# Splitting the routed experts' weights: one copy and one subtraction per chunk, all on ScalarE and VectorE

## The chip, the cores and the metric

The kernel runs on one core of a Trainium2 chip, as one program. The metric is the device time of one execution in microseconds (us), the median of several runs. Traces come from the chip's own profiler, one execution each.

## What is computed

Three layers run one after the other on 2304 tokens of width 512, all in float32: attention with a positive feature map, a dense feed-forward layer, and eight routed experts of which each token takes one. The last matters here:

```python
    expert_idx = np.argmax(logits, axis=1)
    ...
    for e in range(E):
        mask = expert_idx == e
        ...
        h = np.maximum(x[mask] @ w1[e], 0.0)
        out[mask] = gate_w[mask, None] * (h @ w2[e])
```

`w1` is 8 x 512 x 1024 and `w2` is 8 x 1024 x 512.

## The kernel before

**Precision.** TensorE takes operands in a shorter float format (fp32r). To keep float32 accuracy, each operand is split into a rounded part *hi* and the rest *lo* = value - hi, and a product is summed from hi x hi, hi x lo and lo x hi. ScalarE makes hi with a copy that rounds, and a second engine makes lo with a subtraction.

**Stages.** Attention and the first half of the dense layer run block by block (nine blocks of 256 tokens), then the second half of the dense layer, whose blocks also compute the router's scores and pick an expert for each token (`y_half_b`, `route`). From about 610 us on the routed experts run (`run`, `step`). The last routing steps and the building of the late tiles' lists (`make_list`, `list_ids`, `list_tail`) are hooked in between the experts' first steps, since the first five expert tiles come from the tokens that were routed early.

**Tiles and chunks of the experts.** Tokens are sorted by expert into tiles of 128 rows; 23 tiles run in the plain loop, and a further loop for rare distributions follows in a branch. The weights of a tile's expert come in four chunks of 128 x 2048 floats (1 MB): chunks 0 and 1 hold `w1` (used by `up`), chunks 2 and 3 hold `w2` (used by `down`). Each chunk number has one buffer, `raw[c]`. `load_w` (line 805) fills it by an indirect DMA issued on GpSimd's queue (line 797), under a branch that skips the load where the tile has the same expert as the tile before. The load of chunk c for tile i + 1 is issued at the end of `split` of chunk c of tile i, because only then is the buffer free.

**The split (lines 822 to 842).** For each chunk, `split` takes a pair of tiles (hi, lo) out of six pairs that rotate over three pools, and works in two halves of 1024 elements a partition: a ScalarE copy (line 837) for hi, then the subtraction (line 839) for lo. The second half's subtraction goes to GpSimd for chunk 3 of every tile and for chunk 2 of tiles 0, 1 and 2 (`I_POOL`, `C_POOL`, lines 59 and 60); all other halves go to VectorE. The chunks are split in the order (i, 0), (i-1, 2), (i, 1), (i-1, 3), as `chunk_of` gives them.

**A step (line 929).** One tile's step on TensorE: `up(i, 0)` (12 matmuls, as `up(i, 1)` and each `down`), `down(i-1, 0)`, `hT(i, 0)`, `up(i, 1)`, the transposes of the next tile's tokens (`xT`), `down(i-1, 1)`, `hT(i, 1)`; a `split` stands between each two of them. After `up`, ScalarE's relu writes `hs` (line 889); `hT` transposes it on TensorE, ScalarE copies the result (line 899) and VectorE subtracts (line 900). `xT` has such a copy and subtraction as well (lines 790 and 791). GpSimd issues the gather of the next tokens (line 777) and the scatter of results (line 922).

**What orders the work.** TensorE's order is the order of the code (a hand-made schedule), and ScalarE's too in the first two steps. On all other queues a planner places the instructions ahead of time by the times that it assumes; on the chip each engine then works through its list in that order, and an instruction that waits holds up all that stand behind it on its engine.

Of the kernel before, what the change touches and what calls it, by code (L numbers as in the profile page):

```python
# [9 lines left out]
F32 = mybir.dt.float32  # L10
# [45 lines left out]
MAN = (mybir.EngineType.PE,)  # L56
ENDS = (0, 1)
TAILS = ((1, 1), (1, 2), (2, 0), (2, 1))
I_POOL = (0, 1, 2)
C_POOL = (2,)  # L60


@with_exitstack
def tile_attention_moe_router_experts(ctx, tc, qT, kT, va, w_phi, moew, emb, embT, tau, ew, out):
    nc = tc.nc
# [9 lines left out]
    def bc(ap, shape):  # L75
        return ap.to_broadcast(shape)
# [14 lines left out]
    for i in range(2):  # L91
        for r in range(2):
            nc.vector.tensor_copy(
                out=wblk[r * D:(r + 1) * D, i, r * F:(r + 1) * F],
                in_=wstk[r * D:(r + 1) * D, i, :].bitcast(F32),
# [362 lines left out]
    def b_load(j):  # L458
# [23 lines left out]
        out=upper, in_=upper, pattern=[[1, P]], compare_op=ALU.is_gt, fill=0.0, base=0, channel_multiplier=-1  # L482
# [4 lines left out]
    def iota_f(shape, pattern, base_, cm, name):  # L487
# [16 lines left out]
        out=lt8, in0=bc(io8.unsqueeze(2), [P, NE, NE]),  # L504
# [265 lines left out]
    raw = [m1.tile([P, 2048], F32, name=f"raw{c}", bufs=1) for c in range(4)]  # L770
# [34 lines left out]
    def load_w(i, c):  # L805
        if i == 0 or i >= N_PLAIN:
            load_rows(i, c)
            return
        if i not in need:
            need[i] = nc.values_load(  # L810
                lists[i][2], engines=[mybir.EngineType.Pool], min_val=0, max_val=3 * NE
            )
        with tc.If(need[i] < NE):
            load_rows(i, c)

    def chunk_of(k):
        i, s = divmod(k, 4)
        return ((i, 0), (i - 1, 2), (i, 1), (i - 1, 3))[s]
# [3 lines left out]
    def split(k):  # L822
        i, c = chunk_of(k)
        if not span[0] <= i < span[1]:
            return
        n = (k - 2 if k > 3 else k // 2) % 6
        if n == 2:
            pool, tag = xg, "xb"
        elif n == 5:
            pool, tag = ring_c, "W"  # L830
        else:
            pool, tag = ring_b, "W"
        hi = pool.tile([P, 2048], F32R, tag=tag, name="whi")
        lo = pool.tile([P, 2048], F32R, tag=tag, name="wlo")
        for h in range(2):
            hs_ = slice(h * 1024, (h + 1) * 1024)
            nc.scalar.copy(out=hi[:, hs_], in_=raw[c][:, hs_])  # L837
            eng = nc.gpsimd if h == 1 and (c == 3 or (i in I_POOL and c in C_POOL)) else nc.vector
            eng.tensor_sub(lo[:, hs_], raw[c][:, hs_], hi[:, hs_].bitcast(F32))  # L839
        wt_[i, c] = (hi, lo)  # L840
        if i + 1 < span[1]:
            load_w(i + 1, c)
# [86 lines left out]
    def step(i, t0, t1, at):  # L929
        live, prev, more = i < t1, i > t0, i + 1 < t1  # L930
        at(i, 0)
        if 4 * i + LEAD > 3:
            split(4 * i + LEAD)
        if more:
            gather(i + 1)
        if live:
            up(i, 0)
        at(i, 1)
        split(4 * i + 1 + LEAD)
        if prev:  # L940
            down(i - 1, 0)
        if live:
            hT(i, 0)
        at(i, 2)
        split(4 * i + 2 + LEAD)
        if live:
            up(i, 1)
        if more:
            xT(i + 1)
        at(i, 3)  # L950
        split(4 * i + 3 + LEAD)
        if prev:
            down(i - 1, 1)
            finish(i - 1)
        if live:
            hT(i, 1)
# [98 lines left out]
```

## Time and profile before

| | |
|---|---|
| runs before | 957.13, 959.81, 960.24 us, median 959.81 |
| profiled execution | 959.22 us |
| its span, first to last instruction | 957.4 us |
| mean granted TensorE clock | 0.974 |
| busy: TensorE, VectorE, ScalarE, GpSimd | 890.8, 732.1, 571.9, 347.8 us |

The engines are called PE (TensorE), DVE (VectorE), ACT (ScalarE), POOL (GpSimd). A row of a timeline has the start in us from the begin of the span, the length, the engine, the line of the code, the operation, what it writes and reads, how many equal instructions are merged in it, and in brackets how long the engine had been idle and what ended that. The releaser in brackets is inferred, and a wait for several things names the last one only. PEclk is the granted clock as a share of the full one.

### The profile page before, as it was taken

What the parts mean: (1) busy time and instruction counts of PE and PEld (TensorE: products, weight loads), DVE (VectorE), ACT (ScalarE), POOL (GpSimd) and SP (SyncE); (2) the same over time, 40 slices, a digit from 0 to 9 for tenths busy, and PEclk for the clock granted to TensorE, in tenths of its full rate; (3) what the DMA queues carried; (4) which work ended last, traced back from release to release, by engine and by line L of the source; (5) the groups of instructions that cost most, each with busy time, mean ns of one, the idle gap of its engine ahead of it and who ended that gap; (6) DMA issues with size and microseconds to landing.
All of it is one profiled execution on the core that took longest, in us unless ns stands there. A gap on an engine that the chain in (4) does not pass through costs nothing. (4 is left out here: it accounts for less than half of the span.)

```text
span 957.4 us, 18720 instructions
## 1 busy us (share of the span) xinstructions
PE 890.8 (93%) x7144; PEld 763.1 (80%) x7144; DVE 732.1 (76%) x1413; ACT 571.9 (60%) x1048; POOL 347.8 (36%) x267
## 2 busy tenths in 40 slices
PE   7778999999999899789999999997889999999994
PEld 6657988898888788669888898885768887888873
DVE  8998676575746544896888889999988877888860
ACT  6865665474645544553333333477679888988861
POOL 0242122031211311563233224526653666644740
PEclk9879999999999999999999999999899999999998
DMA  8665432232221211563222223412541469411650
GB/s 282 195 185 192 147 85 92 80 116 84 78 91 35 101 67 58 183 211 143 89 89 89 88 89 130 190 34 67 191 184 45 145 210 347 147 38 36 220 186 6
DMA packets 43757, 120.68 MB, mean 126 GB/s; under 512 B 4686, under 2 KB 23246, under 8 KB 36624
## 3 DMA queue, kind: packets, MB, share of 16 engines
q1 hardware_dynamic: 33424, 61.48, 19.8%
q0 software_dynamic: 10160, 57.94, 17.4%
q8 instruction: 57, 0.93, 0.4%
q14 instruction: 36, 0.29, 0.1%
q10 hardware_dynamic: 80, 0.03, 0.0%
HBM read 95.84 MB, written 24.90 MB: 126 GB/s over the span
## 5 line engine op out<-in xcount | busy, mean ns | idle before, releaser
L336 PE MATMUL y<-W,gg 128*128 128x512 f32 x864 | 229.5, 399 | 2.7 <-ACT yt L344 1.6
L839 DVE TENSOR_TENSOR wlo<-raw,whi 128x1024 fp32r<-128x1024 f32 x158 | 201.5, 1307 | 39.3 <-ACT whi L837 39.3
L837 ACT CAST whi<-raw 128x1024 fp32r<-128x1024 f32 x184 | 183.8, 1051 | 52.5 <-DMA raw<-in_ew_dram,lwi 16.2
L336 PEld LDWEIGHTS y<-W,gg 128*128 128x128 f32 x864 | 152.6, 189 | 31.4 <-DVE gg L325 2.1
L315 PE MATMUL h<-xb,W 128*128 128x256 f32 x576 | 166.4, 291 | 11.8 <-DVE g L321 8.0
L316 PE MATMUL h<-xb,W 128*128 128x256 f32 x576 | 164.2, 286 | 0.7 <-DVE xb L269 0.7
L317 PE MATMUL h<-xb,W 128*128 128x256 f32 x576 | 163.5, 285 | 0.0
L227 POOL PARTITION_ALL_REDUCE qmx<-pr x28 | 56.7, 2029 | 210.4 <-ACT pr L209 203.0
L315 PEld LDWEIGHTS h<-xb,W 128*128 128x128 f32 x576 | 109.9, 192 | 22.6 <-DVE g L321 12.0
L316 PEld LDWEIGHTS h<-xb,W 128*128 128x128 f32 x576 | 110.5, 192 | 6.1 <-DVE xb L269 1.3
L317 PEld LDWEIGHTS h<-xb,W 128*128 128x128 f32 x576 | 110.5, 192 | 0.8
L319 ACT ACTIVATE t<-h 128x256 f32<-128x256 f32 x144 | 54.2, 381 | 93.1 <-PE h L317 92.6
L323 ACT CAST gg<-g 128x256 fp32r<-128x256 f32 x144 | 57.3, 404 | 83.9 <-DVE g L321 82.7
L563 DVE CUSTOM_DVE_ANT_0 jk<-ys,enb 128x512 f32<-128x512 f32 x128 | 104.9, 820 | 1.9
L325 POOL TENSOR_TENSOR gg<-g,gg 128x256 fp32r<-128x256 f32 x72 | 58.9, 823 | 123.6 <-ACT gg L323 120.1
L321 DVE TENSOR_TENSOR g<-h,t 128x256 f32<-128x256 f32 x144 | 59.7, 418 | 46.0 <-ACT t L319 44.6
L839 POOL TENSOR_TENSOR wlo<-raw,whi 128x1024 fp32r<-128x1024 f32 x26 | 63.9, 2458 | 58.0 <-ACT whi L837 56.1
L304 POOL TENSOR_TENSOR W<-w,W 128x512 fp32r<-128x512 f32 x32 | 44.6, 1398 | 99.7 <-ACT W L303 99.4
L882 PE MATMUL hps<-whi,xt 128*128 128x512 f32 x184 | 77.2, 420 | 0.0
L912 PE MATMUL yo<-whi,h 128*128 128x512 f32 x184 | 75.4, 410 | 0.0
L913 PE MATMUL yo<-wlo,h 128*128 128x512 f32 x184 | 73.3, 398 | 0.0
L883 PE MATMUL hps<-wlo,xt 128*128 128x512 f32 x184 | 73.2, 398 | 0.0
(212 smaller groups left out, 1742.9 us busy)
## 6 DMA issues: line engine op xcount, KB each, us to landing
wst<-in_moew_dram SPq DMA_DIRECT2D x32, 512.0 KB, 4.8
qraw<-in_q_dram SPq DMA_DIRECT2D x36, 256.0 KB, 3.0
xs_d<-xb SPq DMA_DIRECT2D x9, 1024.0 KB, 4.6
xb<-xs_d POOLq DMA_DIRECT2D x9, 1024.0 KB
kraw<-in_k_dram SPq DMA_DIRECT2D x16, 288.0 KB, 3.7
yp_d<-yt SPq DMA_DIRECT2D x9, 512.0 KB, 2.9
yt<-yp_d SPq DMA_DIRECT2D x9, 512.0 KB, 3.8
y_d<-ys SPq DMA_DIRECT2D x18, 256.0 KB, 2.2
```

What stands on the lines that cost most here:

```text
L315: nc.tensor.matmul(hp, w[:, 0, ks], x[:, 0, k, :], start=(k == 0), stop=False)
L316: nc.tensor.matmul(hp, w[:, 0, ks], x[:, 1, k, :], start=False, stop=False)
L317: nc.tensor.matmul(hp, w[:, 1, ks], x[:, 0, k, :], start=False, stop=(k == 3))
L321: nc.vector.tensor_tensor(out=g, in0=hp, in1=t, op=ALU.max)
L336: nc.tensor.matmul(yps[j][t], gg[:, a, ts], w[:, b, DM:2 * DM], start=(c0 == 0 and a == 0 and b == 0), stop=(c0 == NCH - 1 and a == 1),)
L563: nc.vector.tensor_tensor_reduce(out=jk2, in0=ys, in1=enb[:, e, :], scale=1.0, scalar=0.0, op0=ALU.mult, op1=ALU.add, accum_out=lgr[:, t, ...
L837: nc.scalar.copy(out=hi[:, hs_], in_=raw[c][:, hs_])
L839: eng.tensor_sub(lo[:, hs_], raw[c][:, hs_], hi[:, hs_].bitcast(F32))
L882: nc.tensor.matmul(ps, x[:, 0, k], hi[:, ks], start=(k == 0), stop=False)
L883: nc.tensor.matmul(ps, x[:, 0, k], lo[:, ks], start=False, stop=False)
L912: nc.tensor.matmul(yacc[i], h2[:, 0, k], hi[:, w0], start=(nh == 0 and k == 0), stop=False)
L913: nc.tensor.matmul(yacc[i], h2[:, 0, k], lo[:, w0], start=False, stop=False)
```

## The change

The two halves become one copy and one subtraction for a whole chunk of 128 x 2048. All subtractions go to VectorE; the two constants that chose GpSimd are gone. Nothing else is edited.

```diff
-I_POOL = (0, 1, 2)
-C_POOL = (2,)
...
         hi = pool.tile([P, 2048], F32R, tag=tag, name="whi")
         lo = pool.tile([P, 2048], F32R, tag=tag, name="wlo")
-        for h in range(2):
-            hs_ = slice(h * 1024, (h + 1) * 1024)
-            nc.scalar.copy(out=hi[:, hs_], in_=raw[c][:, hs_])
-            eng = nc.gpsimd if h == 1 and (c == 3 or (i in I_POOL and c in C_POOL)) else nc.vector
-            eng.tensor_sub(lo[:, hs_], raw[c][:, hs_], hi[:, hs_].bitcast(F32))
+        nc.scalar.copy(out=hi, in_=raw[c])
+        nc.vector.tensor_sub(lo, raw[c], hi.bitcast(F32))
         wt_[i, c] = (hi, lo)
```

## Rows read from the trace of the kernel before

**Rows 1.** The page, busy time of each engine, share of the span, instructions.

```profile
PE 890.8 (93%) x7144; PEld 763.1 (80%) x7144; DVE 732.1 (76%) x1413; ACT 571.9 (60%) x1048; POOL 347.8 (36%) x267
```

**Rows 2.** Windows: length, busy time by engine (PE, PEld, DVE, ACT, POOL), PEclk, DMA.

```profile
640.00:660.00 20.00, 17.72 (x96) 14.34 (x95) 19.72 (x29) 19.37 (x26) 11.06 (x5) 1.00 0.09 27
660.00:680.00 20.00, 13.85 (x57) 10.70 (x56) 19.97 (x32) 11.51 (x15) 9.81 (x6) 0.83 0.30 105
680.00:700.00 20.00, 17.00 (x111) 13.33 (x110) 17.26 (x31) 14.53 (x20) 15.24 (x9) 1.00 0.74 264
700.00:720.00 20.00, 17.84 (x126) 14.26 (x126) 17.09 (x24) 14.16 (x19) 9.37 (x6) 0.91 0.37 132
800.00:820.00 20.00, 18.98 (x92) 15.10 (x91) 15.42 (x16) 15.98 (x22) 12.45 (x10) 1.00 0.87 326
860.00:880.00 20.00, 20.00 (x98) 16.34 (x98) 17.02 (x17) 18.12 (x24) 7.07 (x4) 1.00 0.17 54
```

**Rows 3.** Timeline of TensorE, 640 to 745 us: the matmuls after its long waits.

```profile
656.31 0.17 PE L661 MATMUL cnt<-cum,ones 128*128 128x8 bf16 x1 [1.69 <-DVE rk L615]
...
671.44 1.12 PE L896 MATMUL htp<-ident,hs 128*128 128x128 f32 x4 [5.63 <-ACT hs L889]
...
697.22 0.66 PE L896 MATMUL htp<-ident,hs 128*128 128x128 f32 x4 [2.25 <-ACT hs L889]
...
708.54 1.58 PE L886 MATMUL hps<-whi,xt 128*128 128x512 f32 x4 [2.06 <-DVE xt L791]
```

**Rows 4.** Timeline of VectorE, 620 to 745 us: subtractions of line 839, routing operations.

```profile
633.36 2.36 DVE L839 TENSOR_TENSOR wlo<-raw,whi 128x1024 fp32r<-128x1024 f32 x2 [0.21 <-ACT whi L837]
...
638.60 6.73 DVE L839 TENSOR_TENSOR wlo<-raw,whi 128x1024 fp32r<-128x1024 f32 x5 [0.26 <-ACT whi L837]
...
646.14 1.49 DVE L602 TENSOR_TENSOR wt<-lg,mx 128x16 f32<-128x16 f32 x1
...
650.31 2.46 DVE L608 TENSOR_TENSOR cum<-cum,oh 128x8 bf16<-128x8 bf16 x2
...
653.29 2.88 DVE L839 TENSOR_TENSOR wlo<-raw,whi 128x1024 fp32r<-128x1024 f32 x1
...
660.71 1.22 DVE L839 TENSOR_TENSOR wlo<-raw,whi 128x1024 fp32r<-128x1024 f32 x1
...
664.58 2.49 DVE L678 TENSOR_TENSOR ce<-io,inc 128x160 f32<-128x160 f32 x1
...
670.36 2.35 DVE L685 TENSOR_TENSOR same<-ei 128x20 f32<-128x20 f32 x1
...
676.06 0.22 DVE L692 SCALAR_TENSOR_TENSOR lwi<-same,p4c 128x80 int32<-128x80 f32 x1
```

**Rows 5.** Timeline of GpSimd, 606 to 957 us: a subtraction, loads and a scatter.

```profile
645.09 2.51 POOL L839 TENSOR_TENSOR wlo<-raw,whi 128x1024 fp32r<-128x1024 f32 x1 [5.38 <-ACT whi L837]
...
662.75 1.43 POOL L797 DMA_INDIRECT raw<-in_ew_dram,ewi  x1 [5.67 <-PE hps L886]
...
677.54 2.14 POOL L797 DMA_INDIRECT raw<-in_ew_dram,lwi  x1 [4.87 <-ACT whi L837]
679.98 4.27 POOL L922 DMA_INDIRECT out_dram<-o,eoi  x1 [0.30 <-issue]
684.56 1.01 POOL L797 DMA_INDIRECT raw<-in_ew_dram,ewi  x1 [0.31 <-issue]
...
797.60 1.00 POOL L797 DMA_INDIRECT raw<-in_ew_dram,lwi  x1 [0.30 <-DVE wlo L839]
```

**Rows 6.** Timeline of ScalarE, 620 to 745 us: a pair of copies behind a load.

```profile
668.90 1.99 ACT L837 CAST whi<-raw 128x1024 fp32r<-128x1024 f32 x2 [6.56 <-DMA raw<-in_ew_dram,ewi]
```

**Rows 7.** The page, costliest groups: count, busy us, mean ns of one, idle before.

```profile
L839 DVE TENSOR_TENSOR wlo<-raw,whi 128x1024 fp32r<-128x1024 f32 x158 | 201.5, 1307 | 39.3 <-ACT whi L837 39.3
L837 ACT CAST whi<-raw 128x1024 fp32r<-128x1024 f32 x184 | 183.8, 1051 | 52.5 <-DMA raw<-in_ew_dram,lwi 16.2
...
L839 POOL TENSOR_TENSOR wlo<-raw,whi 128x1024 fp32r<-128x1024 f32 x26 | 63.9, 2458 | 58.0 <-ACT whi L837 56.1
```

## The prediction

> **What bounds the kernel now.** I read the page first, then a table of 20 us windows, then the timelines of TensorE, VectorE, GpSimd and ScalarE from 632 us on, where the edited code runs. TensorE is busy for 93% of the span [rows 1], so a change can only give back time in which it waits. The windows show where it waits: not at all in the settled stretch from 860 to 880, where it is busy for 20.00 of 20 us, but for 2.28, 6.15, 3.00 and 2.16 us in the four windows from 640 to 720, 13.6 us together, and for 1.02 us from 800 to 820 [rows 2]. In 640 to 680 VectorE is busy for 39.7 of 40 us: it is the saturated engine while the last tokens are routed and the experts' first tiles already run. So I price the change there, and ask of every gain whether the next late thing swallows it.
>
> TensorE's timeline names four long waits: 1.69 us for a routing operation of VectorE, 5.63 and 2.25 us for ScalarE's relu of the hidden layer (hs), and 2.06 us for VectorE's part of the transposed tokens (xt) [rows 3]. Behind the longest, ScalarE's queue says more than the wait's name: the copy at 668.90 had waited 6.56 us for its weights to land, and the relu stands behind it in the queue [rows 6]. That load was issued at 662.75 [rows 5], 0.8 us after VectorE ended the subtraction that frees the buffer (660.71 + 1.22 us) [rows 4]. Counting the copies in the order of the code, that buffer is chunk 0, subtracted for tile 3 and loaded for tile 4. So VectorE's backlog sets when TensorE resumes at 671.44.
>
> **What the change removes, adds and moves.** *Copies.* Of 184 half copies (1,051 ns each) 92 whole ones are left [rows 7]. No row shows a copy of 2,048 elements a partition. A back-to-back pair takes 1.99 us, of which the second adds about 0.94 [rows 6, 7]: the whole copy lies between twice that, 1.88, and 1.99. I take 1.9, nearer to the low end, since a copy has only one start. ScalarE gains 0.1 us a chunk. In the settled stretch TensorE does not wait, so there it is worth nothing.
>
> *Subtractions on VectorE.* 158 halves become 92 wholes, and 26 halves leave GpSimd (2,458 ns each) [rows 7]. One half undisturbed takes 1.22 us and a pair 2.36 [rows 4], so the second adds 1.14: a whole lies between 2.28 and 2.36. I take 2.3, twice the added part with a little on top. VectorE's total for this line goes from 201.5 us [rows 7] to 92 x 2.3 = 211.6, 10 us more over the stage. In the settled stretch it has 3.0 us of 20 idle [rows 2]: four wholes a tile, 9.2 us, take the place of seven halves on it. A tile has 60 matmuls there (48 with weights, 12 transposes), which at 98 in 20 us [rows 2] is 12.2 us; its three subtractions of 512 elements, estimated at 0.65 us each from the half's 1.22, bring VectorE to about 11.2. The cover of 1 us is thin but in place; if it went, the cost would be up to 1 us a tile.
>
> *Stalls that go.* While GpSimd subtracts, some VectorE operations do not end until GpSimd does. An undisturbed routing operation of 80 elements takes 0.22 us (676.06) [rows 4]. One of 16 took 1.49 at 646.14, ending at 647.63, and the GpSimd subtraction of 645.09 ended at 647.60 [rows 4, 5]. Two of 8 took 2.46 at 650.31, one of 160 took 2.49 at 664.58 and one of 20 took 2.35 at 670.36; a half took 2.88 at 653.29; five halves from 638.60 took 6.73 where 1.22 + 4 x 1.14 = 5.8 [rows 4]. Against undisturbed lengths of about 0.2 us an operation (0.3 for the 160) this is 1.3, 2.1, 2.2, 2.1, 1.7 and 0.9 us. With no subtraction on GpSimd they go.
>
> *Sum to the first checkpoint, TensorE's resumption at 671.44.* VectorE has to get to the end of chunk 0 of tile 3. Gone: 0.9 + 1.3 + 2.1 + 1.7 = 6.0 us. Come: the second halves of four chunks that GpSimd did before it, 4 x 1.14 = 4.6. The other merges save 0.06 us on each of about eight chunks, 0.5. The first subtraction after a wait for ScalarE now starts behind 1.9 us instead of 1.05 us of copy: 0.9 lost once, where VectorE now stands idle only 0.21 us [rows 4]. The merged copy saves 0.1. Sum: -6.0 + 4.6 - 0.5 + 0.9 - 0.1 = -1.1 us.
>
> *GpSimd's queue.* Its loads, gathers and scatters keep their number; they lose the subtractions in front of them. But they also seem to wait for VectorE: the issue at 684.56 took 1.01 us, that at 677.54 2.14, and the scatter at 679.98 4.27, while VectorE subtracted without a pause [rows 5]. With operations of 2.3 instead of 1.2 us the rest of one that an issue meets grows by up to 1.1 us, by 0.5 on average. I add 0.5: the checkpoint moves by -0.6 us. The Trainium skill speaks against this wait: "SBUF — State Buffer", section "Who interferes with whom", infers that a tensor_tensor takes only the read side of the shared ports while descriptor generation needs the write side, so that it would not hold a DMA up. By that rule the checkpoint would move by -1.1; the 4.27 us row disagrees with it.
>
> The wait of 1.69 us goes (its VectorE operation comes about 2 us earlier), and so does any late first chunk: both lie ahead of 671.44, where the landing decides, so both count as nothing.
>
> *Second checkpoint, 697.22.* TensorE waits there for a relu behind copies that waited for another load, issued at 684.56 behind the 4.27 us scatter and the load of 677.54 [rows 3, 5]. That load had to wait for the row numbers of the late tiles, computed on VectorE at 676.06 [rows 4]. On the way there two more stalls go (2.2 + 2.1 = 4.3 us) and two halves come (2.3), with 0.2 of merges: -0.6 - 4.3 + 2.3 - 0.2 = -2.8 us. TensorE arrives early enough, since its small waits for VectorE fall away too. The 2.06 us wait at 708.54 I leave: there one more half takes the place of one more stall.
>
> *Later loads.* From 747 on the experts change often. The load at 797.60 came only 0.30 us after GpSimd's work in front of it [rows 5]; where that holds a subtraction, as it does once a tile, it now goes out up to 2.4 us earlier. Chunks that VectorE did alone free their buffer later: 1.9 + 0.2 + 2.3 = 4.4 us after the copy starts instead of 3.4 (1.05 + 0.2 + 0.94 + 1.22). Between a gain of the 1.02 us [rows 2] and a loss of 1.0 on two or three tiles I take -0.6, since the waiting load is the one that GpSimd held back.
>
> *The first two chunks* are split while the block work before still runs. A whole subtraction there holds one short operation up to 1.1 us longer; two chunks bound it at 0 and +2.2. I take 0, as the 6 us wait behind it covers it; the upper end stays for the range.
>
> **Sum: -2.8 - 0.6 = -3.4 us.** The profiled execution took 959.2 us, 1.8 more than its span of 957.4 and 0.6 less than the median of 959.8. That gives 955.8 on that run and **956.4** against the median.
>
> **Rivals.**
> *VectorE falls behind: slower.* Place: VectorE from 637 to 662. If the stalls are not a cost of the subtractions beside them, but only fall where VectorE had slack, 4.6 us of halves come ahead of the load of 662.75, with the 0.9 and 0.5 above, and TensorE resumes up to 6.0 us later: 959.8 + 6.0 = 965.8. It decides when less than 5.4 us of stalls (6.0 less 0.6 for merges and copy) goes ahead of that load. For it: VectorE is busy for 19.97 of 20 us [rows 2]. Against it: the ends of the stalled operations agree with GpSimd's ends, and I count 6.0. The margin is small, so this keeps 0.23.
>
> *The relief is eaten: no change.* The buffers of chunks 0 to 2 come free 1.0 us later after their copy. If the whole chunk's wait is met two or three times on the path rather than once, at 0.9 each, -2.8 becomes about -1: 959 us. Chance 0.27. That the halves stay halves in effect (the same two columns of work under another name) would look the same.
>
> *A better order: much faster.* The order on ScalarE and VectorE is worked out ahead by a planner. Longer operations can make it place the relu ahead of the copy that waits for a load. Then the 5.63 and 2.25 us waits go and the 1.69 with them [rows 3], 9.6 us, and with the first the slow stretch that follows it: the granted clock of 660 to 680 is 0.83 on average [rows 2], part of it at 1.2 instead of 2.4 GHz, which I estimate at 1 us of matmul time. 959.8 - 10.6 = 949. Nothing in the trace asks for it, so 0.12. The opposite order, more loads ahead of relus, is in the range.
>
> My forecast keeps the remaining 0.38.
>
> **How the numbers follow.** A measurement of this kernel can tell about 0.3%, 2.9 us, from no change. The forecast is a gain of 3.4, close to that bound: of its 0.38, 0.33 lies beyond it; with the better order, 0.45 faster. Within the bound: 0.27 + 0.05 = 0.32. Slower: 0.23. The range runs from 948, a little under the better order, to 965, just short of the slower rival's price; the likeliest case alone has 953 to 959.
>
> **What would show it.** Right: no L839 on GpSimd, 92 whole subtractions at about 2.3 us and 92 copies at 1.9; routing operations of VectorE back at 0.2 to 0.5 us; the load for tile 4 issued before 662.5; VectorE still saturated to about 680, and TensorE at 20.00 of 20 us in the settled stretch. Wrong: a whole subtraction well above 2.36 us; routing operations still at 2 us, with the stalls due to something else; the load issued after 665; TensorE waits in the settled stretch. A copy that waits for a load behind the relu instead of ahead of it would be the planner's work.

## The result: slower by 1.3%, and where the time went

The changed kernel takes 970.91 us (median of 5 runs, 967.43 to 975.66) where the kernel before takes 959.81 (5 runs, 955.59 to 960.62): a ratio of 1.0134 on record, 95% interval 1.0109 to 1.0159 (the quotient of the two medians alone is 1.0116). The forecast was 956.4 us with a range of 948 to 965; sign and range are both wrong. The profiled execution of after took 975.66 us, with a span of 973.9 at a mean granted clock of 0.962. It is the longest of its five runs: against the profiled execution of before its span is 16.5 us longer, while the medians differ by 11.1. Sizes below come from profiles, verdicts from the ratios.

The page of after, busy time and costliest groups, answers to [rows 1, 7]:

```profile
PE 893.9 (92%) x7144; PEld 766.9 (79%) x7144; DVE 734.7 (75%) x1347; ACT 565.1 (58%) x956; POOL 316.9 (33%) x241
...
L834 DVE TENSOR_TENSOR wlo<-raw,whi 128x2048 fp32r<-128x2048 f32 x92 | 211.9, 2303 | 51.6 <-ACT whi L833 51.6
...
L833 ACT CAST whi<-raw 128x2048 fp32r<-128x2048 f32 x92 | 175.5, 1909 | 70.8 <-PE hps L878 26.9
```

The unit prices came out: 2.303 us a subtraction (2.3 was taken) and 1.909 us a copy (1.9). So the instructions cost what they were said to cost, and the time went elsewhere. The windows of after (length, busy time of PE, PEld, DVE, ACT, POOL, PEclk, DMA) show where; before has the same stretches in [rows 2]:

```profile
640.00:660.00 20.00, 12.50 (x71) 10.26 (x69) 18.21 (x17) 16.90 (x15) 3.57 (x2) 0.87 0.08 26
660.00:680.00 20.00, 17.76 (x74) 14.00 (x75) 15.50 (x33) 10.64 (x11) 3.87 (x3) 0.79 0.32 106
680.00:700.00 20.00, 9.81 (x75) 8.01 (x74) 12.88 (x28) 10.40 (x10) 9.99 (x6) 0.81 0.61 224
...
800.00:820.00 20.00, 17.48 (x87) 14.08 (x86) 14.23 (x10) 13.50 (x13) 14.81 (x10) 1.00 0.81 303
820.00:840.00 20.00, 18.07 (x79) 14.31 (x78) 15.52 (x11) 15.37 (x14) 10.78 (x6) 0.91 0.64 237
860.00:880.00 20.00, 20.00 (x98) 16.35 (x97) 17.64 (x12) 17.51 (x16) 5.69 (x3) 1.00 0.16 53
920.00:940.00 20.00, 15.74 (x75) 12.29 (x73) 11.84 (x9) 12.37 (x12) 7.75 (x5) 1.00 0.73 266
```

From 860 to 880 TensorE is busy for 20.00 of 20 us, as before: the thin cover in the settled stretch holds. It idles early (7.50 us in 640 to 660 and 10.19 in 680 to 700, where before idled 2.28 and 3.00; from 660 to 680 it is the other way, 2.24 against 6.15), and late, in the windows where DMA is busy for 0.64 to 0.81 because experts change. The transfers alone do not explain the late part: the run with halves only (x1, below) has a DMA share of 0.85 from 800 to 820, and TensorE is busy for 20.00 us there. The granted clock is lower, too: of the 512-column matmuls of `up` and `down`, 21 in the stretch up to 745 us take 0.6 us or more instead of about 0.39, against 13 before, in lots that follow long waits. Late, 14 more do (seven near 830 us and seven near 943), and none before. TensorE's busy time grows by 3.1 us in all.

To split the loss I take the time at which TensorE starts the first `up` matmul on a *lo* operand of a tile. Tile 7 starts at 734.9 before and 742.7 after (+7.8). From tile 7 to tile 22 before takes 190.4 us and after 198.3 (+7.9). The rest is +0.8. There are two losses of about the same size in these two profiles, and their main causes differ.

**Early: the order on the lists of VectorE and GpSimd.** The timeline of TensorE in after, 645 to 745 us, its long waits:

```profile
660.20 0.19 PE L610 MATMUL prk<-oh,upper 128*128 128x8 bf16 x1 [7.59 <-DVE oh L604]
662.48 0.17 PE L611 MATMUL prk<-cum,ones 128*128 128x8 bf16 x1 [2.04 <-DVE cum L606]
697.23 0.17 PE L733 MATMUL pp<-bw,rm 128*128 128x20 bf16 x1 [9.93 <-DVE bw L717]
```

None of them is a relu, as the longest of before was [rows 3]. All three wait for short routing operations of VectorE. The timeline of VectorE in after, 640 to 700 us:

```profile
646.12 0.17 DVE L585 TENSOR_TENSOR lg<-plg,esc 128x16 f32<-128x16 f32 x1 [1.01 <-PE plg L580]
646.80 2.30 DVE L834 TENSOR_TENSOR wlo<-raw,whi 128x2048 fp32r<-128x2048 f32 x1 [0.51 <-ACT whi L833]
649.01 0.17 DVE L598 TENSOR_REDUCE mx<-lg 128x2 f32<-128x16 f32 x1
...
649.69 2.32 DVE L834 TENSOR_TENSOR wlo<-raw,whi 128x2048 fp32r<-128x2048 f32 x1
651.94 0.16 DVE L600 TENSOR_TENSOR wt<-lg,mx 128x16 f32<-128x16 f32 x1
...
652.62 2.27 DVE L834 TENSOR_TENSOR wlo<-raw,whi 128x2048 fp32r<-128x2048 f32 x1
654.82 0.16 DVE L601 TENSOR_TENSOR wt<-wt,w 128x16 f32<-128x16 f32 x1
654.91 2.28 DVE L834 TENSOR_TENSOR wlo<-raw,whi 128x2048 fp32r<-128x2048 f32 x1
...
657.71 0.15 DVE L603 TENSOR_REDUCE m<-wt 128x2 f32<-128x16 f32 x1
657.79 2.27 DVE L834 TENSOR_TENSOR wlo<-raw,whi 128x2048 fp32r<-128x2048 f32 x1
659.98 0.16 DVE L604 TENSOR_TENSOR oh<-wt,m 128x16 bf16<-128x16 f32 x1
660.07 2.28 DVE L834 TENSOR_TENSOR wlo<-raw,whi 128x2048 fp32r<-128x2048 f32 x1
662.27 0.35 DVE L606 TENSOR_TENSOR cum<-cum,oh 128x8 bf16<-128x8 bf16 x2
...
694.59 2.29 DVE L834 TENSOR_TENSOR wlo<-raw,whi 128x2048 fp32r<-128x2048 f32 x1 [6.55 <-ACT whi L833]
696.80 0.16 DVE L518 TENSOR_SCALAR nr12s<-nr12s 128x6 f32<-128x6 f32 x1
696.87 0.31 DVE L717 TENSOR_SCALAR bw<-bw,pos 128x360 bf16<-128x360 bf16 x1
```

The routing operations are at 0.15 to 0.35 us, with no stall left, as predicted. But they are a chain, each reading what the one before wrote, and the list has one whole subtraction behind each link: six stand between `lg` and `cum`, so that `cum` comes at 662.27, where before had it at 650.31 [rows 4]. Below that, an inversion: the subtraction of tile 5's chunk 0, which waits for weights that land only at about 692.6, stands *ahead of* the last two operations of the lists (`bw`, lines 717 and 718), and TensorE's `pp` waits 9.93 us for them. Between them stands the first operation of the gates (line 518), whose input ScalarE makes behind the same chunk's copy. Before has subtraction and `bw` the other way round (VectorE's timeline of before, 676 to 690 us):

```profile
683.84 0.29 DVE L719 TENSOR_SCALAR bw<-bw,pos 128x360 bf16<-128x360 bf16 x1
684.06 0.52 DVE L720 TENSOR_TENSOR bw<-bw,thr 128x360 bf16<-128x360 bf16 x1
685.37 4.86 DVE L839 TENSOR_TENSOR wlo<-raw,whi 128x1024 fp32r<-128x1024 f32 x2 [0.80 <-ACT whi L837]
```

GpSimd's list is another one, too. Before, the load of tile 5's chunk 0 (677.54) goes ahead of a scatter and of a load for tile 4 [rows 5], and ScalarE's copy of the chunk starts at 684.29. In after it stands behind both (timeline of GpSimd, 640 to 700 us), each of the three is held by a whole subtraction as described under *Late*, and the copy starts at 692.66:

```profile
679.51 2.40 POOL L917 DMA_INDIRECT out_dram<-o,eoi  x1 [6.38 <-ACT o L916]
682.21 2.91 POOL L795 DMA_INDIRECT raw<-in_ew_dram,ewi  x1 [0.30 <-DVE h L895]
685.42 2.44 POOL L795 DMA_INDIRECT raw<-in_ew_dram,lwi  x1 [0.31 <-issue]
```

**Late: GpSimd's issues wait for the subtraction that they meet.** From 745 to 965 us the view of TensorE's waits has one line only, the relu behind a copy (total us, times, longest; before, then after):

```profile
PE htp L896 <- ACT hs L889: 3.1, 4, 1.1
```

```profile
PE htp L891 <- ACT hs L884: 8.9, 4, 3.0
```

Timelines of GpSimd, VectorE, ScalarE and TensorE in after, 922 to 942 us:

```profile
927.99 2.37 POOL L917 DMA_INDIRECT out_dram<-o,loi  x1 [5.84 <-ACT o L916]
930.66 2.55 POOL L795 DMA_INDIRECT raw<-in_ew_dram,lwi  x1 [0.31 <-issue]
935.39 0.99 POOL L795 DMA_INDIRECT raw<-in_ew_dram,lwi  x1 [2.18 <-issue]
...
927.16 2.29 DVE L834 TENSOR_TENSOR wlo<-raw,whi 128x2048 fp32r<-128x2048 f32 x1 [2.63 <-ACT whi L833]
...
930.03 4.58 DVE L834 TENSOR_TENSOR wlo<-raw,whi 128x2048 fp32r<-128x2048 f32 x2
...
937.74 1.90 ACT L833 CAST whi<-raw 128x2048 fp32r<-128x2048 f32 x1 [4.98 <-DMA raw<-in_ew_dram,lwi]
939.55 0.59 ACT L884 ACTIVATE hs<-hps 128x512 f32<-128x512 f32 x1
...
940.19 0.66 PE L891 MATMUL htp<-ident,hs 128*128 128x128 f32 x4 [2.96 <-ACT hs L884]
```

The scatter meets the subtraction that ends at 929.45 (927.16 + 2.29) and ends 0.91 us later, at 930.36. The load behind it meets the first of the two subtractions from 930.03, which ends at 932.32, and ends 0.89 us later, at 933.21. The load at 935.39 meets none and takes 0.99. The weights land at 937.7, the copy, the relu behind it in ScalarE's queue, and TensorE follow, with a wait of 2.96 us. From 720 to 960 us of after, 34 of 57 indirect DMAs start while a subtraction runs. Of these, 33 end 0.83 to 0.91 us after its end and take 1.89 to 3.04 us; one, which starts 0.04 us after its subtraction, is not held. The 23 that meet none take 0.96 to 1.02. Before, with halves, 39 of 57 follow the same rule at 1.16 to 1.84 us; one of all 57 takes over 2 us, against 31 after.

### The profile page after: what moved, and what is told of

Same layout as the page of the kernel before. It is cut to its first block, busy times and chain, and to the rows that moved or that the text cites. A ratio compares the mean times of both kernels' runs of the same rounds, so it can differ in the third digit from the quotient of the medians.

```text
span 973.9 us, 18498 instructions
## 1 busy us (share of the span) xinstructions
PE 893.9 (92%) x7144; PEld 766.9 (79%) x7144; DVE 734.7 (75%) x1347; ACT 565.1 (58%) x956; POOL 316.9 (33%) x241
## 5 line engine op out<-in xcount | busy, mean ns | idle before, releaser
L834 DVE TENSOR_TENSOR wlo<-raw,whi 128x2048 fp32r<-128x2048 f32 x92 | 211.9, 2303 | 51.6 <-ACT whi L833 51.6
L833 ACT CAST whi<-raw 128x2048 fp32r<-128x2048 f32 x92 | 175.5, 1909 | 70.8 <-PE hps L878 26.9
L313 PEld LDWEIGHTS h<-xb,W 128*128 128x128 f32 x576 | 110.1, 192 | 22.4 <-DVE g L319 12.1
L795 POOL DMA_INDIRECT raw<-in_ew_dram,lwi x28 | 50.5, 1804 | 36.0 <-ACT whi L833 9.3
```

What stands on the lines that cost most here:

```text
L313: nc.tensor.matmul(hp, w[:, 0, ks], x[:, 0, k, :], start=(k == 0), stop=False)
L833: nc.scalar.copy(out=hi, in_=raw[c])
L834: nc.vector.tensor_sub(lo, raw[c], hi.bitcast(F32))
```

## Experiments

The theories. *Early*: **links** (each merged subtraction holds one link of the routing chain), with the **inversion** at the lists as a second part; its rival is **load** (VectorE simply has too much to do before tile 7, whatever the order). *Late*: **issue** (longer subtractions lengthen GpSimd's issues); its rival is **buffers** (a whole chunk frees its buffer later). Against all of them stands that the **move** off GpSimd is what costs. The table gathers all runs; ratios are to the kernel before on the same chip (there its median was 957.03 to 957.40), starts are those of the profiled execution in us. Tile 0 starts at 621.9 to 625.9, and x12, whose edit leaves the first six tiles as in before, starts it 2.9 us earlier. Differences of a tile's start hold such shifts, so tile 0 stands beside.

```
kernel                    median  ratio  [95%]            tile 0  tile 4  tile 7  7 to 22  span
before                    959.81                           624.8   689.2   734.9   190.4   957.4
after                     970.91  1.0134 [1.0109, 1.0159]  625.3   704.0   742.7   198.3   973.9
x1 halves, all VectorE    956.77  0.9996 [0.9976, 1.0015]  625.1   698.6   737.4   187.4   956.7
x2 whole to tile 5        961.99  1.0045 [1.0023, 1.0067]  624.8   702.9   741.6   187.6   961.2
x3 whole from tile 6      965.60  1.0102 [1.0075, 1.0128]  622.8   697.4   736.1   191.9   960.8
x4 whole copy, half subs  958.17  1.0016 [0.9999, 1.0033]  625.2   693.4   734.4   187.5   956.3
x8 whole copy, quarters   970.14  1.0140 [1.0113, 1.0166]  624.9   710.3   749.1   188.4   969.7
x5 after, chain first     979.39  1.0244 [1.0219, 1.0269]  625.1   697.4   744.3   192.5   968.9
x6 after, both chains     975.63  1.0208 [1.0180, 1.0236]  625.9   691.9   747.8   193.9   973.5
x7 halves, both chains    965.47  1.0095 [1.0070, 1.0120]  623.3   690.5   742.3   187.7   965.3
x9 after, behind lists    968.87  1.0131 [1.0105, 1.0156]  623.5   696.1   739.0   196.2   967.3
x10 halves, behind lists  952.71  0.9963 [0.9943, 0.9982]  624.1   690.6   730.9   187.5   953.5
x11 x2, behind lists      961.32  1.0038 [1.0018, 1.0057]  624.8   695.8   740.9   187.5   960.0
x12 before, GpSimd early  953.76  0.9978 [0.9958, 0.9999]  621.9   686.3   732.0   187.4   952.2
```

**x1: the move alone.** Copies and subtractions stay halves, all on VectorE.

```diff
-        nc.scalar.copy(out=hi, in_=raw[c])
-        nc.vector.tensor_sub(lo, raw[c], hi.bitcast(F32))
+        for h in range(2):
+            hs_ = slice(h * 1024, (h + 1) * 1024)
+            nc.scalar.copy(out=hi[:, hs_], in_=raw[c][:, hs_])
+            nc.vector.tensor_sub(lo[:, hs_], raw[c][:, hs_], hi[:, hs_].bitcast(F32))
```

> Halves as before, but all of them on VectorE and none on GpSimd: the move without the merge. Theory (links): in the changed kernel each short routing operation stands behind a whole subtraction of 2.3 us in VectorE's list, and the waits for the routing (7.6 + 2.0 us at 652 to 662, 9.9 us at 687 to 697) come from the length of one subtraction. Then halves of 1.2 us bring them down to under 3 us each, and the time is 957 to 962. Rival (load): the 26 halves that GpSimd lost fill VectorE, whatever their size. Then the waits for the routing stay above 5 us each and the time is 967 to 973.

Measured: 0.9996. The move costs nothing on balance, so the 1.34% come from the size. The balance is two terms that cancel: tile 7 comes 2.5 us later than before, and 7 to 22 takes 3.0 us less. The waits are those of neither theory: links had under 3 us each, load above 5 each. The wait at `prk` is shorter than in after (4.25 us) but not gone, and the inversion is there with halves too:

```profile
656.00 0.19 PE L610 MATMUL prk<-oh,upper 128*128 128x8 bf16 x1 [4.25 <-DVE oh L604]
...
692.58 0.18 PE L733 MATMUL pp<-bw,rm 128*128 128x20 bf16 x1 [10.66 <-DVE bw L717]
```

**x2 and x3: whole chunks in one stretch only.** Tiles 0 to 5 whole and the rest halves, and the reverse. The edit against x1:

```diff
-        for h in range(2):
-            hs_ = slice(h * 1024, (h + 1) * 1024)
+        n_ = 2 if i > 5 else 1    # x3: 2 if i <= 5 else 1
+        for h in range(n_):
+            hs_ = slice(h * 2048 // n_, (h + 1) * 2048 // n_)
```

> All on VectorE; whole chunks for tiles 0 to 5, while the routing still runs, halves for tiles 6 to 22. Links: the two waits for the routing stay as in the changed kernel (9.6 and 9.9 us), the waits for the relu after 800 us fall back to about 3 us together: 964 to 969. Rival (buffers: chunks free their buffer later, and the loads of the bursts after 750 come late): most of the loss is in the bursts, so the time falls back to 957 to 962.

> All on VectorE; halves for tiles 0 to 5, whole chunks for tiles 6 to 22. Links: waits for the routing as with halves throughout, waits for the relu after 800 us at 8 to 9 us together as in the changed kernel: about 6 us above the run with halves throughout, 962 to 967. Buffers: all of the loss is here, 967 to 972. Load: no better than the changed kernel either, 967 to 973, but with the waits for the routing above 5 us each.

Measured against x1, by the differences of the ratios: whole chunks early add 0.49% (4.7 us), whole chunks late 1.06% (10 us); together 1.55%, where after has 1.38% over x1. So both stretches lose, and the late one more. x2's time, 961.99, lies in the range of the rival (957 to 962), and x3's, 965.60, in that of links (962 to 967). x2 has after's early waits (7.59, 2.04 and 9.76 us) and 187.6 us from tile 7 to 22, near x1's 187.4. x3's profile is that of its fastest run, 3 us below its median: it shows 191.9 us there, 4.5 more than x1, and too little of the loss.

**x4 and x8: the whole copy stays, the subtraction is cut** into two and four. The buffers come free as late as in after; only the operation that an issue can meet is shorter.

```diff
         nc.scalar.copy(out=hi, in_=raw[c])
-        nc.vector.tensor_sub(lo, raw[c], hi.bitcast(F32))
+        for h in range(2):        # x8: four times 512
+            hs_ = slice(h * 1024, (h + 1) * 1024)
+            nc.vector.tensor_sub(lo[:, hs_], raw[c][:, hs_], hi[:, hs_].bitcast(F32))
```

> One whole copy on ScalarE, two half subtractions, both on VectorE: the merge of the copy alone. Links: VectorE's list can change over after each half, so the waits for the routing are under 3 us each: 957 to 963. Rival (copy): the first half of lo can only start after 1.9 us of copy; if that delay is what the routing and the loads pay for, the time stays at 966 to 973.

> One whole copy, four subtractions of 512 elements, all on VectorE; order left to the planner. Theory (issue): in the bursts GpSimd's load issues wait until the VectorE subtraction that is running ends, so the mean length of an issue follows the subtraction's length: 1.79 us beside whole ones, 1.33 beside halves behind a whole copy, and 1.1 to 1.25 beside quarters; the waits in the bursts are at 2.5 us or less together, though the buffer comes free as late as in the changed kernel (4.3 us after the copy starts). Rival (buffers): the late release alone makes the loads late, the waits in the bursts stay at 5 us or more. Time: 953 to 961 by the first, 962 to 968 by the rival.

Late, this decides it. From the start of the copy to the end of the last subtraction of a chunk it takes 4.24 us on average in after, 4.30 in x4, 4.45 in x8 and 3.45 in x1, yet 7 to 22 takes 198.3, 187.5, 188.4 and 187.4 us. The buffers' rival falls. The issues go with the loss. Groups of instructions on GpSimd, 720 to 960 us (count, busy us, mean ns), the loads, of before:

```profile
L797 POOL DMA_INDIRECT raw<-in_ew_dram,lwi x24 | 31.5, 1311 | 20.8 <-PE htp L896 7.1 <-ACT whi L837 4.3 <-DVE wlo L839 3.1
```

of after:

```profile
L795 POOL DMA_INDIRECT raw<-in_ew_dram,lwi x24 | 43.0, 1792 | 32.4 <-ACT whi L833 9.3 <-DVE h L895 5.4 <-DMA raw<-in_ew_dram,lwi 5.2
```

of x4:

```profile
L795 POOL DMA_INDIRECT raw<-in_ew_dram,lwi x24 | 31.9, 1330 | 34.8 <-DVE xt L789 10.1 <-ACT whi L833 8.3 <-DVE h L897 6.6
```

and of x8:

```profile
L795 POOL DMA_INDIRECT raw<-in_ew_dram,lwi x25 | 31.0, 1242 | 38.5 <-ACT whi L833 14.8 <-ACT h L896 13.3 <-DVE h L897 4.9
```

Early, both surprise: x4's time is what links had, but its wait at `prk` is 7.87 us where they had under 3, and x8's time, 970.14, lies above both ranges. It is as bad as after's, and its loss is nearly all early: tile 7 starts at 749.1, with waits of 10.98 and 14.82 us. All pieces of a chunk become ready with its one copy, and the list takes them together: between `lg` and `oh` x8 has six lots of four quarters, and x4 five pairs of halves. So cutting the operation alone does not shorten the chain. What differs is the inversion. x4 does not have it: `bw` is done at 688.9, ahead of the subtraction of 689.31, and `pp` waits 0.79 us. Its tile 7 starts at 734.4, as early as before's. x8 has it: the quarters of 699.46, which had waited 10.01 us, stand ahead of `bw` (702.56). Their weights are late: on GpSimd the scatter and the load ahead of theirs (680.31 and 683.68) took 3.07 and 5.62 us beside lots of quarters. TensorE's timeline of x4 shows its two waits:

```profile
660.53 0.19 PE L610 MATMUL prk<-oh,upper 128*128 128x8 bf16 x1 [7.87 <-DVE oh L604]
...
688.53 0.17 PE L733 MATMUL pp<-bw,rm 128*128 128x20 bf16 x1 [0.79 <-DVE bw L717]
```

**x5, x6, x7: let the chains go first.** The planner is told to place subtractions behind the last operation of the first routing chain (x5, from tile 2's chunk 0 up to tile 9), and from tile 3's chunk 0 on behind the lists (x6; x7 with halves). The edit of x5:

```diff
+    held = [None, None]
...
-            nc.vector.tensor_add(cum[:, t + 1, :], cum[:, t, :], oh[:, t, :])
+            held[0] = nc.vector.tensor_add(cum[:, t + 1, :], cum[:, t, :], oh[:, t, :])
...
+        m = held[0] if 8 <= k < 40 else None
         nc.scalar.copy(out=hi, in_=raw[c])
-        nc.vector.tensor_sub(lo, raw[c], hi.bitcast(F32))
+        with tc.issue_after(m.ins) if m else nullcontext():
+            nc.vector.tensor_sub(lo, raw[c], hi.bitcast(F32))
```

> The changed kernel, with the subtractions of line 834 that are traced behind the last block's routing queued on VectorE behind the last operation of its first chain (scores to running counts); nothing else moves. Theory (links): five or six whole subtractions stand between the chain's operations in the changed kernel, 2.3 us each, and they alone make TensorE wait 7.6 + 2.0 us at 652 to 662. With them behind the chain these waits fall under 2 us. The second chain (lists) is still threaded, so its wait of about 10 us may stay: 962 to 969. Rival (load): VectorE has too much to do in any order, the wait comes back at the next operation that TensorE needs, and the time is 968 to 973.

> As the run before, and from tile 3's first chunk on the subtractions queue behind the last operation of the lists' chain too. Links: both long waits (9.6 and 9.9 us) fall to under 3 us each; what stays of the loss are the waits for the relu in the bursts after 800 us (8.9 us in the changed kernel against 3.1 before): 951 to 962. Load: VectorE catches up later at the price of as long waits for chunks, 966 to 973.

> The kernel with all halves on VectorE, with both chains ahead of the subtractions in the same way. Links: the waits for routing of 4.3, 1.6 and 10.7 us fall to under 3 us each and nothing comes in the bursts (0.4 us there): 943 to 952, under the kernel before. Load: 955 to 960, as without the reordering.

Measured: slower than what they start from, by 1.1, 0.7 and 1.0%. The wait at `prk` goes, and others come in its place: in x5 one of 5.96 us for a relu at 673.04, and one of 6.12 at `pp`. That subtractions which are held free their buffers later, so that the next weights land later and the relu behind their copy is late, is the likely way; no run isolates it. The links' numbers were missed three times. What load expects, that an early wait only changes its name, fits, but its times were passed, too (at most 973, 973 and 960 us), and VectorE is not short of time: from 640 to 700 us of after it is busy for 46.6 of 60 us. x5's profiled run is its fastest, 8.8 us under its median, so its late part is not read.

**x9, x10, x11: undo the inversion alone.** Only the subtractions from tile 5's chunk 0 on, and the first operation of the gates, are placed behind the lists' last operation; in after (x9), x1 (x10) and x2 (x11). The edit of x9:

```diff
+    held = [None, None]
...
-        nc.vector.tensor_scalar(out=s, in0=s, scalar1=1e-30, scalar2=None, op0=ALU.max)
+        with tc.issue_after(held[1].ins) if after else nullcontext():
+            nc.vector.tensor_scalar(out=s, in0=s, scalar1=1e-30, scalar2=None, op0=ALU.max)
...
-        nc.vector.tensor_tensor(
+        held[1] = nc.vector.tensor_tensor(
...
+        m = held[1] if 20 <= k < 40 else None
         nc.scalar.copy(out=hi, in_=raw[c])
-        nc.vector.tensor_sub(lo, raw[c], hi.bitcast(F32))
+        with tc.issue_after(m.ins) if m else nullcontext():
+            nc.vector.tensor_sub(lo, raw[c], hi.bitcast(F32))
```

> The changed kernel, with two things queued on VectorE behind the last operation of the late tiles' lists: the subtractions from chunk 0 of tile 5 on, and the first operation of the gates. Theory (inversion): the wait of 9.9 us at 687 to 697 is there because the list has tile 5's subtraction, whose weights have not landed, ahead of the lists' last operations. Then this wait falls under 1 us; TensorE next waits for the relu that stands behind tile 5's copy on ScalarE, so that not all of it comes back: tile 7 starts about 3 to 6 us earlier than at 742.7, the time is 963 to 968. Rival (capacity: VectorE has more to do in this stretch than it can, in any order): the wait comes back in full elsewhere, tile 7 starts at 742 or later, 970 to 975.

> The same edit in the kernel with all halves on VectorE (wait for the lists there 10.7 us, tile 7 starts at 737.4). Inversion: the wait falls under 1 us, tile 7 starts at 732 to 736, the time is 950 to 956. Capacity: tile 7 at 737 or later, 957 or more.

> The same edit, whole chunks for tiles 0 to 5, halves from tile 6 on: without the late issues in the bursts. Inversion and issue together leave little of the loss: 954 to 960. If one of the two is not a cause, 962 or more.

Measured: the wait at `pp` falls to 1.20, 0.88 and 1.20 us. What that is worth differs. With halves tile 7 starts 6.5 us earlier (737.4 to 730.9), of which 1.0 was there at tile 0, and x10 has the lowest ratio of the study, 0.9963, its interval clear of 1. With whole chunks tile 7 gains 3.7 us in x9, of which 1.8 was there at tile 0, and 0.7 in x11; their ratios (1.0131, 1.0038) can't be told from those of after and x2, and their times (968.87 and 961.32) fall between the two ranges on record. With whole chunks most of the 9.9 us therefore returns elsewhere. VectorE's list in x10 around the lists, timeline 676 to 692 us:

```profile
680.95 0.32 DVE L720 TENSOR_SCALAR bw<-bw,pos 128x360 bf16<-128x360 bf16 x1
681.18 0.53 DVE L721 TENSOR_TENSOR bw<-bw,thr 128x360 bf16<-128x360 bf16 x1
686.77 2.36 DVE L841 TENSOR_TENSOR wlo<-raw,whi 128x1024 fp32r<-128x1024 f32 x2 [5.07 <-ACT whi L839]
```

The subtraction still idles 5.07 us for its weights, but the lists no longer stand behind it.

**x12: the useful half of the move.** Before, with GpSimd's subtractions kept in tiles 0 to 5 only.

```diff
-            eng = nc.gpsimd if h == 1 and (c == 3 or (i in I_POOL and c in C_POOL)) else nc.vector
+            eng = nc.gpsimd if h == 1 and i <= 5 and (c == 3 or (i in I_POOL and c in C_POOL)) else nc.vector
```

> The kernel before, with GpSimd's subtractions kept for tiles 0 to 5 only; halves throughout, from tile 6 on all on VectorE. If GpSimd's subtractions cost the bursts (waits of 3.1 us there before, 0.4 with all halves on VectorE) and nothing else changes, tiles 7 to 22 take 187.4 us instead of 190.4: 953 to 957, 2 to 4 us under the kernel before. If they cost nothing: 956 to 960, no difference.

Measured: 0.9978, faster than before with 0.9999 as the upper end of the interval; 7 to 22 takes 187.4 us, as in x1, and tile 0 to tile 7 takes 110.1, as before. What the move gives late, 3.0 us, is had without what it costs early.

## Why the prediction was wrong

**Copies and subtractions, unit prices: right**, 1.909 and 2.303 us. **Settled stretch: right**, 20.00 of 20 us. **Stalls that go: right** as far as the operations are concerned, 0.15 to 0.35 us each.

**"Sum to the first checkpoint" and "Second checkpoint": wrong.** The sum gave -2.8 us and tile 7 starts 7.8 us later. Its terms were added along the list of before. That list is not given; the planner makes it anew from the changed instructions. It put six whole subtractions between the links where before had two halves on VectorE between 645.3 and 650.3 us, it put tile 5's first subtraction ahead of the last list operations, and it put the load for that subtraction third on GpSimd. The prediction counted the wait for a routing operation, 1.69 us before, as gone and worth nothing; the waits for such operations came to 7.59, 2.04 and 9.93 us. The prediction names the planner's order only as a favourable rival ("A better order", 0.12) and dismisses the opposite ("in the range"). What the sum was made for did move: the load for tile 4 ended its issue at 663.27 (660.89 + 2.38), 0.9 us before the 664.18 of before [rows 5], where -0.6 was forecast. But TensorE no longer waits for it. The row numbers of the late tiles, behind the second checkpoint, came at 681.00 instead of 676.06 [rows 4], 4.9 us later where -2.8 was forecast, since whole subtractions stand between their links, too. Timelines of GpSimd and VectorE in after, 640 to 700 us:

```profile
660.89 2.38 POOL L795 DMA_INDIRECT raw<-in_ew_dram,ewi  x1 [5.07 <-DVE oh L604]
...
681.00 0.22 DVE L690 SCALAR_TENSOR_TENSOR lwi<-same,p4c 128x80 int32<-128x80 f32 x1
```

How much of the 7.8 us each part has stays open: x4 keeps the `prk` wait and loses nothing by tile 7, x10 gains 6.5 us without the inversion, but x9 and x11 gain 3.7 and 0.7, and x5 to x7 lose. That order costs is shown by x10 against x1, where nothing but the order is edited: from tile 0 to tile 7 it takes 106.8 us instead of 112.3. With whole chunks the held issues stand in the way early, too: the copy of tile 5's chunk 0 starts at 691.05 in x9 and at 685.69 in x10, behind a scatter and two loads that take 2.38, 2.91 and 2.46 us in x9 and 2.16, 1.62 and 1.00 in x10. No run separates that part from the order.

**"GpSimd's queue": right in kind and size, applied once instead of everywhere.** The prediction put 0.5 us on a load's issue, in part from a row that does not bear it: at 684.56, where it has VectorE subtract without a pause, VectorE stands idle until 685.37, so the 1.01 us there is the undisturbed length. The loads' mean went from 1.31 to 1.79 us, 0.48 more. But it charged one checkpoint, and for **"Later loads"**, the second term that failed, it took -0.6, where 7 to 22 came out at +7.9. Two things were overlooked. Every load *and* the scatter or gather ahead of it can meet a subtraction, so the delays add: in the stretch shown, 1.4 and 1.6 us. And where an expert changes the loop of copy, subtraction, issue, landing and the next copy has no slack: from one copy of a chunk number to its next it takes 12.93 us in before, 13.72 in after and 12.38 in x1 (means over the 24 late loads), against the 12.5 us that TensorE's settled step takes. A delay there is paid on each of the tiles that load. The gain that the prediction saw is real: x1 and x12 have 3.0 us from GpSimd's subtractions leaving the loads' queue, five times the 0.6 that was taken. The whole subtraction takes back 4.5 (x3) to 10.9 us (after). The prediction had the step (12.2 us there), but not the loop's length beside it; what it costed was the later release of the buffer, which x4 and x8 show to be harmless.

The Trainium skill, "SBUF — State Buffer", section "Who interferes with whom", infers that such a subtraction would not hold up a DMA's issue. By that rule the late loss would not exist. The runs disagree: in after 33 issues end 0.83 to 0.91 us after the subtraction that they met and take 1.89 to 3.04 us, where an issue that meets none takes 1.0.

**Rivals.** "VectorE falls behind: slower" had the sign, but not the mechanism: the stalls were a cost of the subtractions beside them (the routing operations are back at 0.15 to 0.35 us), and its price of +6.0 is not what happened at that place. "The relief is eaten" fits x1, not the change. The condition that would have shown the prediction wrong, TensorE waiting in the settled stretch, did not occur; the waits are before it and in the bursts of loads, and the list of signs named no wait there. One sign of being right failed: VectorE, which was to stay saturated to about 680, is busy for 15.50 of 20 us from 660 to 680. Some 9 of its 39.7 us before, from 640 to 680, were the stalls that the prediction lists.

## What to carry to other kernels

Where a planner orders the queues, merging two instructions is also a new order: ask which short dependent operations share the list with the merged one, and which instruction that waits for a transfer could come to stand ahead of them. A price per issue has to be multiplied by the loads whose loop has no slack, and it counts for each DMA in the queue ahead of the load, too. Cut the work in the pieces that suit the neighbour: here halves on VectorE throughout, with the lists placed first, or GpSimd's help in the early tiles only, came out 0.4 and 0.2% under the kernel before.

## What was not expected of the hardware

An indirect DMA that GpSimd starts while VectorE subtracts with two operands in on-chip memory ends, in most cases, 0.83 to 0.91 us after that one operation, whether it has 512, 1024 or 2048 elements a partition: from 720 to 960 us, 33 of 34 in after, 39 of 41 before, 29 of 40 in x8. Beside whole subtractions back to back it ends while the second runs (933.21, above). Mean lengths of the loads' issues follow: 1.24 us beside quarters, 1.31 to 1.47 beside halves (before, x1, x4, x10) and 1.79 to 1.85 beside whole ones (after, x3). Some issues beside quarters and halves took longer than one operation: of x8's in that stretch, 9 of 40 ended 1.4 us or more after the first, and one ahead of it, at 683.68, took 5.62 us. What decides this is not shown.

TensorE pays for a long wait twice. After the 7.59 and 2.04 us of waiting that end at 662.48, matmuls of 512 columns take 0.63 us for some 5 us, and then 0.39 (timeline of TensorE in after, 645 to 700 us):

```profile
663.08 0.63 PE L878 MATMUL hps<-wlo,xt 128*128 128x512 f32 x1
...
668.70 0.39 PE L907 MATMUL yo<-whi,h 128*128 128x512 f32 x1
```

The granted clock of the windows there is 0.87 and 0.79 on average: a mean of the level of 1.2 GHz and that of 2.4.
